# A gate projection by Strassen's algorithm on pairs of batches, with key and gate weights converted to float32 ahead of it

## The chip, the cores and the metric

One Trainium2 chip, of which the kernel uses one core. The time is device microseconds of one launch. TensorE (PE in the rows) multiplies matrices, VectorE (DVE), ScalarE (ACT) and GpSimd (POOL) work elementwise, and SyncE (SP) issues nearly all transfers from one queue.

## What is computed

Attention over 4 batches, 12 heads, 448 tokens and head width 64; then a mixer over tokens and channels; then the block that the change is about, here cut down:

```python
xk = mu_k * x + (1.0 - mu_k) * x_prev
xr = mu_r * x + (1.0 - mu_r) * x_prev
k = np.maximum(xk @ w_k, 0.0)
v = k * k @ w_v
r = 1.0 / (1.0 + np.exp(-(xr @ w_r)))
return (r * v).astype(np.float32)
```

`x` is 4 x 448 x 768, `x_prev` the same moved by one token. `w_r` is 768 x 768, `w_k` 768 x 1024 and `w_v` 1024 x 768. The weights arrive as 64-bit floats. The product with `w_r` is the gate, that with `w_k` the keys, that with `w_v` the values.

## The kernel before, in words

Every float32 operand of a large product is held as a high part (rounded) and a low part (the rest), and every block product is three matmuls: high by high, high by low, low by high (`mm3`, lines 542 to 544). Making the two parts, a split, costs one copy on ACT (`high`, L408, or L596 for the gate's inputs) and one subtraction on DVE (`low`, L412, or L599). A block of 64-bit weights is turned into float32 by one instruction on ACT (L357, or L277 in the attention part) and three on DVE (L362, L369 and L376, or L282, L289 and L295).

The program has two phases, each put in order by a list scheduler written out in the file (`walk`): each step carries an engine, an estimated cost, what it reads and writes and a due time, and the scheduler emits the instructions engine by engine. Nothing is reordered on the chip: each engine takes its own list, and SP's transfers go out in the order of SP's list.

- Phase 0 is attention with token mixing for 24 pairs of heads; idle PE time is filled with the first channel-mixing products (`pd`).
- Phase 1 begins with channel mixing (`ph`, `acc`). Its outputs `u` (L648) are blended with the previous token (L666 on ACT, L670 on DVE) for keys and for gate and stored to `x_d`.
- The gate follows. For each of two pairs of batches there are 14 units of 128 tokens by 384 columns (12 of whole 128-token tiles, 2 of the remaining 64 tokens of both batches), each a sum over six blocks of 128 channels: `pr`, 28 units of 18 matmuls. The inputs of a batch are loaded (L677), split in place (L596, L599), and the remaining tokens copied aside by a transfer (L706). The sigmoid (L718) reads PSUM and the result is parked in `r_d`.
- The keys (`pk`) and values (`pv`) already use Strassen's algorithm: 7 block products for 8, with sums of blocks formed on DVE (`take`, L400) before a split, and the products summed out of PSUM on DVE (L779, L858).
- Weights for the gate and keys are converted just ahead of and during the gate; those of the values are converted in channel mixing, combined, parked in `s_d` as float32 and loaded again in the keys.

The lines that set the gate's work per matmul and its size:

```python
def unit(o, n, x, w, start, stop):
    cs = slice(HALF * (n % 2), HALF * (n % 2 + 1))
    mm3(o[:, :HALF], [((x[:, 0], x[:, 1]), (w[:, 0, cs], w[:, 1, cs]))], start, stop)
...
    for p in range(B // 2):
        for n in range(14):
```

Of the kernel before, what the change touches and what calls it, by code (L numbers as in the profile page):

```python
# [10 lines left out]
F32 = mybir.dt.float32  # L11
# [9 lines left out]
def kernel(  # L21
# [66 lines left out]
    s_d = dpool.tile([28, 128, 384], F32, name="s_d")  # L88

# [31 lines left out]
    def walk(mine, rank):  # L121
# [218 lines left out]
    chain = {}  # L340

    def load64(t, key, src, n, own=None, blocks=False):
# [30 lines left out]
        def assemble():  # L373
# [5 lines left out]

        k = object()  # L380
        g = n / 384
        u = [("raw", k), (own or "tmp", k)]
        last = chain.get("last")
        chain["last"] = (("raw", k), key)
        op(t, SP, dma(128 * n * 8), load, r=[last[0]] if last else [], w=[("raw", k)], u=u[:1])
        op(
            t, ACT, 0.04 + 0.41 * g, magnitude, r=[("raw", k)] + ([last[1]] if last else []),
# [30 lines left out]

    FORMS = ("11", "s2", "12", "s3", "s1", "22", "s4")
# [3 lines left out]
    def w_place(fam, blk, i):  # L423
        return 4 * {"v": BLOCKS, "k": FORMS}[fam].index(blk) + i

# [11 lines left out]
    def v_weight(t, dt, kt):  # L437


        def get(t, blk, row, col, own=None):  # L440
            src = w_v[row * 128:(row + 1) * 128, 384 * col:384 * (col + 1)]
            return load64(t, ("wf", blk, kt), src, 384, own)

        def done(t, blk, tile):
            def store():
                nc.sync.dma_start(s_d[w_place("v", blk, kt)], tile[0]())

            op(
                t, SP, dma(128 * 384 * 4), store, r=[("wf", blk, kt)], w=[("ws", blk, kt)],
                u=[tile[1]],  # L450
            )

        def sub(t, blk, o, x, y, r):
            r = [("wf", b, kt) for b in r] + [("ws", b, kt) for b in blk[1:]]
            take(t, ("wf", blk[0], kt), r, [o[1], x[1], y[1]], o[0], x[0], y[0])

        a = get(t, "11", kt, 0, "tma")
        done(t, "11", a)
        b = get(t + dt, "12", kt, 1, "tmb")
        sub(t + dt, ("t1", "11"), a, b, a, ("12",))  # L460
        done(t + dt, "t1", a)
        c = get(t + 2 * dt, "22", kt + KF // 2, 1)
# [5 lines left out]
        d = get(t + 3 * dt, "21", kt + KF // 2, 0)  # L468
# [4 lines left out]
    def v_reload(t, dt, r):  # L473

        for n in range(28):
            blk, kt = BLOCKS[n // 4], n % 4
            tag = ("tma", "tmb")[n % 2]
            box, own = {}, (tag, ("re", n))

            def load(n=n, tag=tag, box=box):  # L480
                box["t"] = L["tv"].tile([128, 384], F32, tag=tag, name="tmp")
                nc.sync.dma_start(box["t"], s_d[n])

            op(
                t, SP, dma(128 * 384 * 4), load, r=[("ws", blk, kt)] + (r if n < 2 else [("rl64", n - 2)]),
                w=[("rl64", n)], u=[own],
            )
            split32(
                t + 2, ("W", "v", blk, kt), [("rl64", n)], [w_slot("v", blk, kt), own],
                lambda blk=blk, kt=kt: w_half("v", blk, kt), lambda box=box: box["t"],  # L490
# [3 lines left out]
    def k_weight(t, dt, q):  # L494


        def get(t, blk, row, col, own=None):
            src = w_k[384 * row:384 * (row + 1), 128 * (q + 4 * col):128 * (q + 4 * col + 1), :]
            src = src.rearrange("(c p) m w -> p c m w", p=128)
            return load64(t, ("kf", blk, q), src, 384, own, True)  # L500

        def done(t, blk, tile):
            split32(
# [4 lines left out]
        def add(t, blk, o, x, y, r, d, plus=False):  # L508
            r = [("kf", b, q) for b in r] + [("W", "k", b, q) for b in d]
            take(t, ("kf", blk, q), r, [o[1], x[1], y[1]], o[0], x[0], y[0], plus=plus)  # L510

        a = get(t, "21", 0, 1, "tma")
        b = get(t + dt, "11", 0, 0, "tmb")
        done(t + dt, "11", b)
        c = get(t + 2 * dt, "22", 1, 1)
# [7 lines left out]
        d = get(t + 3 * dt, "12", 1, 0)  # L523
# [23 lines left out]
    JA = 8  # L547
# [6 lines left out]
    def ch_weight(n, t, dt, pool):  # L554
# [6 lines left out]
    L = {}  # L561
    NB_ = KF * 2 + KD - NPRE
    bufs.update({
        "a2": KD, "a3": 2, "z": 7, "tma": 1, "tmb": 1, "rot": 2, "rp": 7,
# [3 lines left out]
    def open_late():  # L568
# [4 lines left out]
        new("a2", bufs=KD)  # L573
        new("a3", bufs=2)
        new("tv", bufs=1)
        new("zp", bufs=7)
# [73 lines left out]
    xs, rs, ks, rest, at, duo, xpool = {}, {}, {}, {}, {}, {}, {}  # L650
# [24 lines left out]
    def r_in(b, m):  # L675
        xs[1, b, m] = hl(xpool[1, b])
        nc.sync.dma_start(raw(xs[1, b, m]), x_d[1, b, m])  # L677

    def r_hi(b, m):
        part_hi(xs[1, b, m])  # L680

    def r_lo(b, m):
        part_lo(xs[1, b, m])
# [4 lines left out]
    def unit(o, n, x, w, start, stop):  # L688
        cs = slice(HALF * (n % 2), HALF * (n % 2 + 1))
        mm3(o[:, :HALF], [((x[:, 0], x[:, 1]), (w[:, 0, cs], w[:, 1, cs]))], start, stop)  # L690

    def tokens(n):
        return slice(128 * (n % 6 // 2), 128 * (n % 6 // 2 + 1))

    def bank(p, n):
        return f"acc{(14 * p + n) % KD}"

    def new_bank(p, n):
        rs["p", p, n] = L["acc"].tile([128, 512], F32, tag=bank(p, n), name="pr")

    def gate_rest(p, i, c):
        if ("x", p, c // 3) not in rest:
            rest["x", p, c // 3] = hl("a3")
        o = rest["x", p, c // 3][:, :, 128 * (c % 3):128 * (c % 3 + 1)]
        rest[1, p, c] = o
        nc.sync.dma_start(  # L706
            o[:, :, 64 * i:64 * i + 64].bitcast(F32), xs[1, duo[p][i], c][:, :, 384:].bitcast(F32)
        )
# [7 lines left out]
    def gate_out(p, n):  # L716
        rs[p, n] = L["rp"].tile([128, S], F32, tag="r", name="r")
        nc.scalar.activation(rs[p, n][:, :HALF], rs["p", p, n][:, :HALF], AF.Sigmoid)  # L718

    def gate_store(p, n):  # L720
        nc.sync.dma_start(r_d[p, n], rs[p, n][:, :HALF])
# [154 lines left out]
    def channel_mixing():  # L876
# [3 lines left out]
        W0, W1 = 150, 6  # L880
        V0, V1, K0, K1 = 140, 22, 40, 20
# [32 lines left out]
        for t, (b, kind, j) in enumerate(beats):  # L914
# [15 lines left out]
            if b != B - 1 and j < JA:  # L930
                op(
                    t - 3.2 * BEAT, SP, dma(SB), h_load, b, j, r=[("h_d", b, j), seen[-4]],
# [42 lines left out]
        GU, VU = 3.15, 4.2  # L975
        T3 = T2 + 14 * GU * B // 2
        N2 = 2 * KF * BEAT + 14 * VU
        at_w = {}
        for c in range(KD):
            key = ("r", c)  # L980
            at_w[key] = free_slots[c]
            weight(T2 - W0 + W1 * c, W1 / 2, at_w[key], w_r, False, c, key)
        r_slots, k_slots = free_slots[:KD], free_slots[KD:KD + 14]
        t1_slot.append(free_slots[KD + 14])
        u2_slots.extend((free_slots[KD + 15], r_slots[0]))
        for i in range(14):
            w_use["k", i] = (k_slots[i], ("W", "k", i))
        v_slots = r_slots[1:] + k_slots[:9]
        for i in range(14):
            w_use["v", i] = (v_slots[i], ("W", "v", i))  # L990
        RING = [t1_slot[0]] + k_slots[9:] + u2_slots
        KP = 7 * 4 * 3 * 0.61
        T4 = T3 + 2 * KP
        for q in range(4):
            v_weight(T2 - V0 + V1 * q, V1 / 4, q)
        for q in range(4):
            k_weight(T2 - K0 + K1 * q, K1 / 4, q)
        v_reload(T4 - 80, 2.2, [("W", "k", f, q) for f in FORMS for q in range(4)])

        rounds = [(1, b) for b in batches] + [(0, b) for b in batches]  # L1000
        gone = [
            ("ch1", batches[-1], KC - 1, KD - 1), ("c2", batches[-1], KC - 1, 0),
            ("gl", 0, 5), ("gl", 0, 11), ("gl", 1, 5),
        ]
        for n, (i, b) in enumerate(rounds):
            if i:
                xpool[i, b] = ("ue", "a2")[n % 2]
            t0 = T2 + 7 * GU * n if i else T3 + KP * (n - B) // 2
            for m in range(KD):
                need = [("x_d", i, b, m)]  # L1010
                if i or at[b][0] == 0:
                    need.append(gone[min(n, B)])
                else:
                    need.append(("km", 0, "s1", 0, 0))
                if not i:
                    t = T3 + KP * at[b][0] - 35 + 2 * m + at[b][1]
                    x = ("ue", "kx", at[b][0], m)
                    op(t, SP, dma(SB), k_in, b, m, r=need, w=[("yt", i, b, m)], u=[x])
                    continue
                t = t0 - 190 + 3 * m  # L1020
# [758 lines left out]
```

## Time and profile before

| | us |
|---|---|
| three runs | 906.22, 906.80, 911.61; median 906.8 |
| the profiled execution | 906.09, of which 904.1 are the span from the first to the last instruction |
| attention (with the first channel-mixing products) | 0 to 343 |
| channel mixing | 343 to 605.5 |
| gate | 605.5 to 692.9 |
| keys | 692.9 to 797.1 |
| values and the end | 797.1 to 904.1 |

The page counts 892.8 us of the span as busy on PE, 628.4 on DVE and 507.7 on ACT; its lines of forty digits give PE 9 in every slice but the first and the last, and the granted TensorE clock as 9 (full) in all of them. A matmul's busy time overlaps the next one's, so the pace of the matmuls has to be read from their starts.

### The profile page before, as it was taken

To read this page: it belongs to the slowest core of one execution; us is meant where nothing else is said; L and a number is where in the kernel's file an instruction comes from. 1 tells how busy PE (TensorE), PEld (TensorE's weight loads), DVE (VectorE), ACT (ScalarE), POOL (GpSimd) and SP (SyncE) were. 2 spreads that over 40 slices of the span, in tenths; PEclk is the share of its full clock that TensorE was granted. 3 is DMA by queue.
4 is the path that set the end of the run, shared out by engine and by line. 5 is a ranking of instruction groups with operands and counts; after the bars stand their busy time and mean duration, and the time that the engine had idled before them with its cause. 6 is when DMAs were issued, how large, how long until landed. Compare 5 with 4: busy or idle time off the path is not lost.

```text
span 904.1 us, 15752 instructions
## 1 busy us (share of the span) xinstructions
PE 892.8 (99%) x5340; PEld 802.9 (89%) x5340; DVE 628.4 (70%) x1568; ACT 507.7 (56%) x1205; POOL 47.8 (5%) x125
## 2 busy tenths in 40 slices
PE   7999999999999999999999999999999999999997
PEld 4688888888888889999999999999999999999997
DVE  6899997683576436887986557479723676888773
ACT  7988886674667444545554324366524576753330
POOL 1302111110101000000000000000000000000000
PEclk9999999999999999999999999999999999999999
DMA  9646755533242103666785785748762444576642
GB/s 189 171 122 162 213 165 165 151 83 93 69 133 63 51 32 113 186 186 231 254 293 195 252 295 184 228 141 282 232 226 90 154 164 141 189 231 194 181 144 62
DMA packets 174129, 151.66 MB, mean 168 GB/s; under 512 B 87584, under 2 KB 166944, under 8 KB 174048
## 3 DMA queue, kind: packets, MB, share of 16 engines
q1 hardware_dynamic: 173120, 150.42, 55.0%
q8 instruction: 42, 0.69, 0.3%
q10 hardware_dynamic: 928, 0.23, 0.1%
q14 instruction: 39, 0.32, 0.1%
HBM read 103.16 MB, written 45.88 MB: 165 GB/s over the span
## 4 chain that ended last, share of the span: by engine, by line
PE 94%; ACT 3%; DVE 1%; DMA 1%; issue 0%; SPq 0%
PE acc L544 6%; PE acc L542 6%; PE acc L543 6%; PE pv L1467 5%; PE pe L1451 4%; PE ph L542 4%; PE ph L544 4%; PE ph L543 4%; PE pk L544 4%; PE pk L543 4%; PE pk L542 4%; PE pv L544 4%; PE pv L543 4%; PE pv L542 4%; PE ps L1382 3%; PE pd L542 3%
## 5 line engine op out<-in xcount | busy, mean ns | idle before, releaser
L1410 ACT ACTIVATE e<-ms,nm 112x336 f32<-112x336 f32 (+3 forms) x192 | 100.5, 530 | 12.5 <-DVE nm L1394 11.7
L543 PE MATMUL acc<-a,w 128*128 128x448 f32 x288 | 105.2, 365 | 0.0
L542 PE MATMUL acc<-a,w 128*128 128x448 f32 x288 | 105.2, 365 | 0.0
L544 PE MATMUL acc<-a,w 128*128 128x448 f32 x288 | 105.2, 365 | 0.0
L1394 DVE CUSTOM_DVE_ANT_0 ms<-ps,mask 112x448 f32<-112x448 f32 (+3 forms) x192 | 76.7, 442 | 27.3 <-PE ps L1382 22.4
L542 PE MATMUL pv<-wv,kk 128*128 128x384 f32 x196 | 65.5, 334 | 0.0
L544 PE MATMUL pv<-wv,kk 128*128 128x384 f32 x196 | 65.5, 334 | 0.0
L543 PE MATMUL pv<-wv,kk 128*128 128x384 f32 x196 | 65.5, 334 | 0.0
L599 DVE TENSOR_TENSOR a<-a 128x448 fp32r<-128x448 f32 x84 | 51.0, 627 | 19.1 <-ACT a L596 19.0
L246 ACT COPY et<-pe 112x448 f32<-112x448 f32 x104 | 50.9, 540 | 21.5 <-PE pe L1451 21.4
L543 PE MATMUL pk<-a,wk 128*128 128x448 f32 x168 | 61.8, 368 | 0.0
L544 PE MATMUL pk<-a,wk 128*128 128x448 f32 x168 | 61.8, 368 | 0.0
L542 PE MATMUL pk<-a,wk 128*128 128x448 f32 x168 | 61.8, 368 | 0.0
L596 ACT CAST a<-a 128x448 fp32r<-128x448 f32 x84 | 46.0, 567 | 24.7 <-DMA a<-h_d 20.2
L1451 PE MATMUL pe<-ident,e 112*112 112x112 f32 x480 | 57.6, 261 | 0.9 <-ACT qt L1352 0.5
L542 PEld LDWEIGHTS acc<-a,w 128*128 128x128 f32 x288 | 54.1, 188 | 4.3
L543 PEld LDWEIGHTS acc<-a,w 128*128 128x128 f32 x288 | 54.1, 188 | 4.3
L544 PEld LDWEIGHTS acc<-a,w 128*128 128x128 f32 x288 | 54.1, 188 | 4.3
L542 PE MATMUL pd<-a,w 128*128 128x448 f32 x144 | 57.4, 399 | 0.0
L408 ACT CAST kk<-a 128x512 fp32r<-128x512 f32 x49 | 30.2, 620 | 48.4 <-PE pv L544 41.7
L1451 PEld LDWEIGHTS pe<-ident,e 112*112 112x112 f32 x480 | 49.3, 133 | 8.6 <-issue 2.0
L543 PE MATMUL pr<-w,a 128*128 128x384 f32 x168 | 56.1, 334 | 0.0
(137 smaller groups left out, 2226.9 us busy)
## 6 DMA issues: line engine op xcount, KB each, us to landing
raw<-in_moe_w_ch_dram SPq DMA_DIRECT2D x48, 384.0 KB, 3.4
x_d<-t SPq DMA_DIRECT2D x48, 224.0 KB, 3.5
a<-x_d SPq DMA_DIRECT2D x48, 224.0 KB, 4.5
a<-u_d SPq DMA_DIRECT2D x36, 224.0 KB, 3.8
raw<-in_moe_w_v_dram SPq DMA_DIRECT2D x16, 384.0 KB, 3.9
raw<-in_moe_w_k_dram SPq DMA_DIRECT2D x16, 384.0 KB, 4.2
a<-a_d SPq DMA_DIRECT2D x24, 256.0 KB, 4.4
vn<-in_v_dram SPq DMA_DIRECT2D x48, 112.0 KB, 2.7
```

The source lines that it names most:

```text
L246: nc.scalar.copy(o, i) if by == ACT else nc.vector.tensor_copy(o, i)
L408: nc.scalar.copy(dest()[0], src())
L542: nc.tensor.matmul(o, lh, rh, start=start and i == 0, stop=False, skip_group_check=skip)
L543: nc.tensor.matmul(o, lh, rl, start=False, stop=False, skip_group_check=skip)
L544: nc.tensor.matmul(o, ll, rh, start=False, stop=stop and i == n - 1, skip_group_check=skip)
L596: nc.scalar.copy(t[:, 0], raw(t))
L599: nc.vector.tensor_sub(t[:, 1], raw(t), t[:, 0].bitcast(F32))
L1382: nc.tensor.matmul(T["s", j, c], T["q"][r, x, qc], T["k"][r, y, :n], start=i == 0, stop=i == 2,)
L1394: nc.vector.tensor_tensor_reduce(out=ms[:, :n], in0=T["s", j, c], in1=mask[:, S - n:], scale=-0.125, scalar=BIG, op0=ALU.add, op1=ALU.min, ...
L1410: nc.scalar.activation(T["e", j][:, eoff[c]:eoff[c + 1]], T["ms", j, c][:, :n], AF.Exp, bias=T["nm"][:, j, c:c + 1], scale=-1.0, accum_out ...
L1451: nc.tensor.transpose(pe[:CP, o + (c - kc) * CP:o + (c - kc + 1) * CP], T["e", j][:, eoff[c] + kc * CP:eoff[c] + (kc + 1) * CP], ident[:CP ...
L1467: nc.tensor.matmul(T["pv"][64 * j:64 * j + 64, kc * CP:S], T["vn"][:, kc, j, :], T["et"][:, o:o + S - kc * CP], start=kc == 0, stop=kc == 2,)
```

## The change

The gate is computed on pairs of batches by Strassen's algorithm. A product of two batches' rows with `w_r` cut into two by two blocks takes 7 block products. The 14 tiles of 128 tokens form 7 groups of two ("quads"): three from the first pair of batches, three from the second, and one of the remaining 64 tokens of all four. Each block product of a quad is three blocks of 128 channels, so 9 matmuls; a pass over three quads is 27 matmuls per product. The inputs of a pair are loaded as plain float32, summed on DVE (`take`, now L409), and each of the seven forms is split into its own tile (L417 on ACT, L421 on DVE). Five of the seven products need a sum out of PSUM on DVE (`r_sum`, L831), the first a copy on ACT (`r_copy`, L828). The pool of split tiles (`a2`) has 8 in place of 6, that of the blended tiles (`z`) 6 in place of 7, and four single tiles (`tma` to `tmd`) serve the weights in place of two.

24 blocks of weights (8 of the gate's 12, all 16 of the keys') are converted in the attention part by `convert`, from the eleventh pair of heads on and with a late due time, and stored as float32 in `c_d`; later they are fetched from there. The last four blocks of the gate's weights are still converted in channel mixing. Half of the keys' weight forms (14 of 28) are made earlier than before, parked in `t_d` and loaded again late (`reload`).

The core of the diff:

```diff
+    t_d = dpool.tile([14, 128, 384], F32, name="t_d")
+    c_d = dpool.tile([24, 128, 384], F32, name="c_d")
...
+    def convert(t, fam, blk, i, gate):
+        n = early[fam, blk, i] = len(early)
+        tile, own = load64(t, ("cf", n), block_src(fam, blk, i), 384, None, fam == "k", gate)
+        def store():
+            nc.sync.dma_start(c_d[n], tile())
+        op(t, SP, dma(128 * 384 * 4), store, r=[("cf", n)], w=[("cd", n)], u=[own])
...
-        "a2": KD, "a3": 2, "z": 7, "tma": 1, "tmb": 1, "rot": 2, "rp": 7,
+        "a2": A2, "z": 6, "tma": 1, "tmb": 1, "tmc": 1, "tmd": 1, "rot": 2, "rp": 7,
...
+    def r_bank(n, q, where):
+        if n == REST:
+            return "rot"
+        return f"acc{q + (3 if where == 'b' else 0)}"
+    def rmm(n, f, q, c):
+        blk, where, start, stop = PRODUCTS[f]
...
+        mm3(
+            rp_[n, q, where][:, :HALF], [((x[0][:, cs], x[1][:, cs]), w_half("r", blk, c))],
+            start=start and c == 0, stop=c == KD // 2 - 1, skip=not start,
+        )
+    def r_sum(n, q, o, where, x):
+        nc.vector.tensor_add(r_temp(n, q, o), rp_[n, q, where][:, :HALF], r_temp(n, q, x))
...
-    def gate(p, n, c):
-        if c == 0:
-            new_bank(p, n)
-        x = xs[1, duo[p][n // 6], c][:, :, tokens(n)] if n < 12 else rest[1, p, c]
-        unit(rs["p", p, n], n, x, weights["r", c]["t"], c == 0, c == KD - 1)
...
+        def x_tile(gone):
+            n = len(xs_free)
+            xs_free.append(gone)
+            return xs_free[n - KD] if n >= KD else [("ch1", batches[-1], KC - 1, KD - 1)]
...
+                    m, x = len(cols) * half + c, ("ue", "rx", n, len(cols) * half + c)
+                    gone = x_tile([("ro", n, f, c) for f in (("s4", "22") if half else ("s2", "s3"))])
...
+                add(t, "s1", ld((0, 1), (1, 1)), s1, a21, a22, True)
+                add(t + 0.2, "s3", made("s1") + ld((0, 0)), a21, a11, a21)
+                add(t + 0.4, "s2", made("s3") + [("ro", n, "11", c)], a11, s1, a11)
+                add(t + 0.6, "s4", made("s2") + ld((1, 0)) + [("ro", n, "12", c)], a12, a12, a11)
...
+        GATE, LOW = 10, 60
...
+        blocks = [("r", b, i) for i in (1, 2) for b in ("11", "12", "22", "21")]
+        blocks += [("k", b, i) for i in range(4) for b in ("21", "11", "22", "12")]
+        for i, x in enumerate(blocks):
+            g = GATE + i * (NP * B - 1 - GATE) // len(blocks)
+            convert(tp(g) + LOW, *x, [("xlo", g)])
```

What stands where on the engines that PE waits for shows at two places. The first is DVE right behind the last channel-mixing output (`u`, the row that ends at the first gate matmul). Before, the splits of the gate's inputs and the making of the keys' weights stand there:

```order
L648 TENSOR_TENSOR u_7249<-acc5_6889,u_7249 128x448
...
L369 TENSOR_SCALAR tmp_7348<-tmp_7348 128x384
L599 TENSOR_TENSOR a_7371<-a_7371 128x448
L400 TENSOR_TENSOR tmp_7269<-tmp_7291,tmp_7269 128x384
L412 TENSOR_TENSOR wk_7199<-tmp_7322,wk_7199 128x384
L400 TENSOR_TENSOR tmp_7291<-tmp_7322,tmp_7291 128x384
L412 TENSOR_TENSOR wk_7206<-tmp_7269,wk_7206 128x384
L376 SCALAR_TENSOR_TENSOR tmp_7348<-raw_7296,tmp_7348 128x384
```

Behind the change it is splits of Strassen forms (`a_7531` and so on), sums out of PSUM (`pr`) and the blends, 62 rows from here to the split of the third column of the second pair's first form:

```order
L734 TENSOR_TENSOR u_7448<-acc5_7059,u_7448 128x448
L421 TENSOR_TENSOR a_7531<-a_7289,a_7531 128x448
L756 SCALAR_TENSOR_TENSOR t_7460<-u_7419,mu_r_75,t_7460 128x448
L756 SCALAR_TENSOR_TENSOR t_7472<-u_7427,mu_r_75,t_7472 128x448
L421 TENSOR_TENSOR a_7569<-a_7304,a_7569 128x448
...
L409 TENSOR_TENSOR s1_7900<-a_7633,a_7848 128x448
L409 TENSOR_TENSOR a_7633<-a_7633 128x448
L831 TENSOR_TENSOR x_7587<-pr_7653,x_7587 128x384
L409 TENSOR_TENSOR a_7633<-s1_7900,a_7633 128x448
...
L831 TENSOR_TENSOR x_7644<-pr_7832,x_7644 128x384
L421 TENSOR_TENSOR a_7902<-a_7748,a_7902 128x448
```

The conversions of 64-bit weights (L362, L369, L376) are gone from this place, and the forms of the second pair (`s1_7900` on) stand ahead of the split `a_7902` that its first product needs.

The second place is SP's list in the gate. Before, the loads of the third batch stand together, with the raw weights:

```order
L349 DMA raw_7296<-in_moe2_w_k_dram 128x3x256
L677 DMA a_7302<-x_d_78 128x448
L677 DMA a_7308<-x_d_78 128x448
L677 DMA a_7314<-x_d_78 128x448
L677 DMA a_7317<-x_d_78 128x448
L677 DMA a_7334<-x_d_78 128x448
L349 DMA raw_7339<-in_moe2_w_k_dram 128x3x256
```

Behind the change the second half of the second pair's inputs (`a_7848`, `a_7863`, `a_7875`, two transfers each) stands behind stores of the first pair's gate (`r_d`):

```order
L759 DMA x_d_78<-t_7792 128x448
L839 DMA r_d_79<-w_7758 128x384
L774 DMA a_7848<-x_d_78 128x448 x2
L774 DMA a_7863<-x_d_78 128x448 x2
L774 DMA a_7875<-x_d_78 128x448 x2
L839 DMA r_d_79<-w_7781 128x384
```

These tiles are taken over from the first pair, so each pair of loads also waits until the first pair's fourth form (`s4`) of the same column has been split.

## Rows read from the trace of the kernel before

**Rows 1.** The page's part 4: shares of the chain that ended last, by engine.
```profile
PE 94%; ACT 3%; DVE 1%; DMA 1%; issue 0%; SPq 0%
```

**Rows 2.** Busy time by stage: stretch, length; PE, PEld, DVE, ACT, POOL; clock, DMA share, GB/s.
```profile
174.00:343.00 169.00, 169.00 (x1223) 143.42 (x1220) 97.93 (x327) 105.06 (x294) 10.80 (x27) 1.00 0.28 82
343.00:572.00 229.00, 229.00 (x1132) 212.26 (x1131) 166.14 (x355) 102.56 (x201) 4.56 (x36) 1.00 0.68 220
...
605.50:692.90 87.40, 87.40 (x505) 87.39 (x505) 53.56 (x108) 43.42 (x88) 0.50 (x5) 1.00 0.64 209
692.90:797.10 104.20, 104.20 (x506) 94.66 (x506) 70.08 (x125) 69.50 (x137) 0.00 (x0) 1.00 0.53 170
```

**Rows 3.** What PE waited for, whole span: first and last of six rows.
```profile
PE pt L1348 <- DMA kn<-in_k_dram: 4.0, 1, 4.0
...
PE ps L1373 <- DVE nm L1394: 0.2, 1, 0.2
```

**Rows 4.** PE in order of time at both ends of the gate: start, length, instruction.
```profile
605.32 0.36 PE L544 MATMUL acc<-a,w 128*128 128x448 f32 x1
605.52 0.34 PE L542 MATMUL pr<-w,a 128*128 128x384 f32 x1
...
692.73 0.33 PE L544 MATMUL pr<-w,a 128*128 128x384 f32 x1
692.90 0.36 PE L542 MATMUL pk<-a,wk 128*128 128x448 f32 x1
```

**Rows 5.** The page's part 5: one of the gate's three matmul lines.
```profile
L543 PE MATMUL pr<-w,a 128*128 128x384 f32 x168 | 56.1, 334 | 0.0
```

**Rows 6.** DVE in order of time around the gate's start: start, length, instruction, count.
```profile
602.68 3.66 DVE L648 TENSOR_TENSOR u<-acc,u 128x448 f32<-128x448 f32 x6 [1.18 <-DMA a<-x_d]
606.26 2.76 DVE L599 TENSOR_TENSOR a<-a 128x448 fp32r<-128x448 f32 x5
...
612.07 0.55 DVE L412 TENSOR_TENSOR wk<-tmp,wk 128x384 fp32r<-128x384 f32 x1
612.54 0.55 DVE L400 TENSOR_TENSOR tmp<-tmp 128x384 f32<-128x384 f32 x1
...
616.41 1.27 DVE L670 SCALAR_TENSOR_TENSOR t<-u,mu_r,t 128x448 f32<-128x448 f32 x2
```

**Rows 7.** DVE in the gate by line and form: count, busy us, mean ns, idle before.
```profile
L599 DVE TENSOR_TENSOR a<-a 128x448 fp32r<-128x448 f32 x18 | 10.5, 619 | 2.1 <-ACT a L596 2.1
...
L376 DVE SCALAR_TENSOR_TENSOR tmp<-raw,tmp 128x384 int32<-128x384 int32 x9 | 5.0, 555 | 0.2
L670 DVE SCALAR_TENSOR_TENSOR t<-u,mu_k,t 128x448 f32<-128x448 f32 x6 | 4.0, 678 | 0.1
...
L362 DVE TENSOR_SCALAR tmp<-tmp 128x384 f32<-128x384 f32 x9 | 3.2, 354 | 3.1 <-ACT tmp L357 3.1
```

**Rows 8.** The same in the values: a sum out of PSUM.
```profile
L858 DVE TENSOR_TENSOR u<-pv,x 128x384 f32<-128x384 f32 x14 | 7.8, 556 | 7.4 <-PE pv L544 7.4
```

**Rows 9.** ACT in the gate by line and form.
```profile
L596 ACT CAST a<-a 128x448 fp32r<-128x448 f32 x15 | 8.0, 561 | 0.1
```

**Rows 10.** SP's queue in order of time: six loads of gate inputs.
```profile
569.84 3.36 SPq L677 DMA_DIRECT2D a<-x_d  x6
```

**Rows 11.** Transfers issued in the gate: KB each, median us to landing.
```profile
a<-x_d SPq DMA_DIRECT2D x25, 224.0 KB, 5.1
```

**Rows 12.** Transfers issued at the end of channel mixing, the same columns.
```profile
a<-x_d SPq DMA_DIRECT2D x12, 224.0 KB, 3.8
```

**Rows 13.** The tile of natural keys in attention: first and last start, time to landing.
```profile
L1348 PE MATMUL pt<-ident,kn x96: 257/259/421, 4.0 to 289.0; 112*128 112x112 f32 x96
L1337 SPq DMA_DIRECT2D kn<-in_k_dram x47: 312/481/2298, 0.7 to 274.0; - x47
...
DMA to landing us min/median/max: 2.0/3.4/5.0
```

**Rows 14.** What SP's queue waited for from 174 to 343: total, times, longest.
```profile
SPq L1697 <- ACT he L1694: 52.9, 12, 8.4
```

More of the change, by code (lines that the diff above doesn't have):

```diff
@@ L338, in weight, with load64 @@
             t += dt
-    chain = {}
-    def load64(t, key, src, n, own=None, blocks=False):
+    chain, DEEP = {}, 2
+    def load64(t, key, src, n, own=None, blocks=False, gate=()):
         box = {}
@@ L378, in assemble @@
             )
+        held = [] if own else [chain[x] for x in ("tma", "tmb", "tmc", "tmd") if x in chain]
+        if own:
+            chain[own] = key
         k = object()
@@ L382, in load64 @@
         u = [("raw", k), (own or "tmp", k)]
-        last = chain.get("last")
-        chain["last"] = (("raw", k), key)
-        op(t, SP, dma(128 * n * 8), load, r=[last[0]] if last else [], w=[("raw", k)], u=u[:1])
+        last = chain.setdefault("last", [])
+        was = last[-DEEP] if len(last) >= DEEP else None
+        last.append((("raw", k), key))
+        op(t, SP, dma(128 * n * 8), load, r=list(gate) + list(was[:1] if was else []), w=[("raw", k)], u=u[:1])
         op(
-            t, ACT, 0.04 + 0.41 * g, magnitude, r=[("raw", k)] + ([last[1]] if last else []),
+            t, ACT, 0.04 + 0.41 * g, magnitude, r=[("raw", k)] + ([was[1]] if was else []) + held,
             w=[("mag", k)], u=u,
@@ new lines, in r_in, with r_s1 @@
+    def r_in(n, m, i):
+        if n != REST:
+            nc.sync.dma_start(r_block(n, m, i), x_d[1, duo[n][i], m])
+            return
+        o = r_block(n, m, i).rearrange("p (c t) -> p c t", t=128)
+        for e in range(2):
+            src = x_d[1, duo[i][e], 3 * m:3 * m + 3, :, 384:]
+            nc.sync.dma_start(o[:, :, 64 * e:64 * e + 64], src.rearrange("c p t -> p c t"))
+    def r_s1(n, c):
+        if (n, "s1") not in rx:
+            rx[n, "s1"] = pools[t1_slot[0]].tile([128, 2, 768], F32R, tag=t1_slot[0], name="s1")
+        t = rx[n, "s1"].rearrange("p a b -> p (a b)").bitcast(F32)
+        return t[:, :HALF] if n == REST else t[:, S * c:S * (c + 1)]
@@ new lines, in r_form @@
+    def r_form(n, f, c):
+        if (n, f, c) not in ro:
+            ro[n, f, c] = hl("a2")
+        t = ro[n, f, c]
+        return (t[:, 0, :HALF], t[:, 1, :HALF]) if n == REST else parts(t)
+    def r_bank(n, q, where):
[4 more added lines that the diff above has]
+        blk, where, start, stop = PRODUCTS[f]
+        if start and c == 0:
+            b = r_bank(n, q, where)
+            rp_[n, q, where] = (
+                L["rot"].tile([128, 512], F32, tag="r", name="pr") if b == "rot"
+                else L["acc"].tile([128, 512], F32, tag=b, name="pr")
+            )
+        x = r_form(n, f, 0 if n == REST else c)
+        cs = slice(128 * (c if n == REST else q), 128 * (c if n == REST else q) + 128)
+        mm3(
+            rp_[n, q, where][:, :HALF], [((x[0][:, cs], x[1][:, cs]), w_half("r", blk, c))],
+            start=start and c == 0, stop=c == KD // 2 - 1, skip=not start,
+        )
@@ new lines, in r_temp @@
+    def r_temp(n, q, name):
+        if (n, q, name) not in rz:
+            if n == 0 and name in "xu":
+                slot = r_room[name]
+                if (n, slot) not in rz:
+                    rz[n, slot] = pools[slot].tile([128, 2, 768], F32R, tag=slot, name="x")
+                t = rz[n, slot].rearrange("p a b -> p (a b)").bitcast(F32)[:, HALF * q:]
+            elif name in "xu":
+                t = ytile(name, "zp")
+            else:
+                t = L["rp"].tile([128, S], F32, tag="r", name=name)
+            rz[n, q, name] = t[:, :HALF]
+        return rz[n, q, name]
@@ L716, in gate_out @@
[L716 to L721, printed above, removed]
     def gate_load(p, n):
@@ new lines, in channel_mixing @@
+        RP = 7 * (KD // 2) * 0.53
+        T3 = T2 + 7 * RP
+        KP = 7 * 4 * (KD // 2) * 0.61
+        T4 = T3 + 2 * KP
+        r_slots, k_early = free_slots[:11], free_slots[12:22]
+        t1_slot.append(free_slots[11])
+        u2_slots.extend(r_slots[4:6])
+        late = [w_place("k", f, q) // 2 for f, q in LATE[6::2]]
+        k_slots = [None] * 14
+        for i, x in enumerate([i for i in range(0, 14, 2)] + [i for i in range(1, 14, 2) if i not in late]):
+            k_slots[x] = k_early[i]
```

392 lines of the change are left out of this document (249 added, 143 removed), and 5 rows, old and new, of the table NUDGES.

## The prediction, written before the change was run

> **What bounds the kernel now.** The first view is the chain that ended last: 94% of it is PE [rows 1], so a gain must take work off PE, or a loss must make PE wait. The second is the table by stage: from 174 us on PE is busy in the whole of every stretch shown, at a granted clock of 1.00 [rows 2], while DVE is busy 98 of 169 us in late attention, 166 of 229 in channel mixing, 54 of 87 in the gate. Since busy time hides gaps, the third view is what PE waited for: six rows between a 4.0 us wait for the first keys and one of 0.2 us [rows 3], about 6 us in all, every one at lines of attention. The fourth is PE in order of time at both ends of the gate: the last channel-mixing matmul starts at 605.32 and the gate's first at 605.52, the last at 692.73 and the keys' first at 692.90 [rows 4]. So the gate takes 692.90 - 605.52 = 87.4 us for 3 x 168 = 504 matmuls [rows 5], one every 87.4 / 504 = 0.1734 us, with no gap at either end. PE alone bounds it.
>
> I count time from the gate's first matmul, called zero.
>
> **What the change takes off PE.** Seven quads of 7 products of 9 matmuls are 441 for 504. Their shape is the same, 128 x 128 by 384 columns, so the pace should be too: 441 x 0.1734 = 76.5 us, 10.9 less. Against the profiled execution of 906.1 that is 895.2. The median of the runs is 0.7 above that execution, which I add at the end.
>
> **What it puts on DVE in the gate.** First the price of a row. Five splits of 448 columns take 2.76 us together and one lasts 0.62 [rows 6, 7], so they start (2.76 - 0.62) / 4 = 0.535 apart; two rows of 384 columns start at 612.07 and 612.54, 0.47 apart though each lasts 0.55; two blends start 1.27 - 0.68 = 0.59 apart [rows 6, 7]. A sum out of PSUM of 384 columns lasts 0.556 [rows 8], like the other 384-wide rows, so I put it at 0.47 too (an estimate).
>
> In the new order, from the last output `u` to the last sum of the gate, DVE has 138 rows: 66 of 448 columns, 12 blends, 60 of 384 columns (35 sums out of PSUM, 25 others). 66 x 0.535 + 12 x 0.59 + 60 x 0.47 = 70.6 us, in a gate of 76.5. Before, it was busy 53.6 of 87.4 [rows 2]. DVE goes from 61% to over 90%, and that is where the change can fail. The gate's inputs were split once (24 tiles); now there are 49 splits of forms and 28 sums of blocks, and 35 sums of products that did not exist. What is saved are raw conversions (two rows of 0.35 and one of 0.56 for a block [rows 7]).
>
> Two splits are tight. The 26th row is that of the third column of form `s3`. The 26 rows take 8 x 0.535 + 9 x 0.59 + 9 x 0.47 = 13.8 us. The first row behind `u` starts 0.74 after zero (606.26 [rows 6]), so it ends at 14.6; PE wants it at its 90th matmul, 89 x 0.1734 = 15.4. It is in time by 0.8.
>
> The 62nd is `a_7902`, the third column of the second pair's first form. 28 x 0.535 + 12 x 0.59 + 22 x 0.47 = 32.4, plus 0.74: 33.1. PE wants it at its 198th matmul, at 34.2: 1.0 to spare, if DVE never waits. It will, twice. Row 49 sums product `22` of the second quad, which PE ends at 26.5, so rows 49 on cannot be before 27.2. Row 50 needs the second pair's inputs `a_7848`, whose tile is free once `s4` of that column is split, the 42nd row, at 23.0. SP issues such loads 0.56 apart (six in 3.36 [rows 10]), so the second of the two leaves at 23.7; landing took 3.8 us at the end of channel mixing [rows 12] and 5.1 in the gate [rows 11]. Row 50 thus starts between 27.5 and 28.8, and the 13 rows from it to `a_7902` take 9 x 0.535 + 4 x 0.47 = 6.7: it ends between 34.2 and 35.5, so PE is late by 0 to 1.3 us. I take 1.1, near the upper end, since the 5.1 is from the same stage, though the keys' raw loads of 384 KB no longer fall into it. Later splits have 3 us and more, in the last quad 12, since work on PE outlasts that on DVE. The three sums that free the banks for the second pair lie among the 62 rows and are due later or at the same time.
>
> ACT makes one copy for each of 62 splits (0.56 [rows 9]) and has 47 other rows, sigmoids of 384 columns for the most part; at 0.56 for each that is at most 61 of 77 us, under DVE's load and off the path.
>
> **What it puts elsewhere.** Attention gets 24 conversions, each one row on ACT, three on DVE (0.35 + 0.35 + 0.56 [rows 7]), a raw load and a store: 30 us on DVE and some 13 on ACT. DVE has 71 us free from 174 to 343 alone, ACT 64, and the transfer engines are 0.28 busy there [rows 2]. PE's own instructions are the same 2352 before the first `acc`, with a few exchanged places. I cost it at nothing; what hides it is this free time and the lead of the loads below. Channel mixing loses the gate's conversions and gains sums, splits and stores; in its last three batches DVE's rows grow by some 6 us of 175, with 63 free in the row of 229 us [rows 2]: nothing. In the keys, eight blocks of weights arrive only after the gate's weights are done with. The first of them is for the fourth product, and a product there lasts 104.2 / 14 = 7.4 us [rows 2], so they have 22 us for loads that land in 5.1: nothing.
>
> **Sum.** 906.1 - 10.9 + 1.1 = 896.3 against the profiled execution, **897.0** against the median.
>
> **Rivals.**
> *DVE falls behind in the gate.* If a row on DVE started only when the one before it had ended, the 62 rows would take 28 x 0.62 + 12 x 0.68 + 22 x 0.555 = 37.7 us, `a_7902` would end at 38.5 and PE would stand 4.3 us: 900.2 against the median. Rows of 0.55 that start 0.47 apart speak against it. [...] The likelier way to the same place is inputs that land later than 5.1, or a blend that waits for one of only six `z` tiles, with DVE's list held up behind it; 3 to 7 us lost give 899 to 903.5. Together 0.20.
>
> *Attention starves for its loads: slower.* The 24 stores of converted blocks stand in SP's one list, each waiting for DVE's last row of a low-priority conversion, and the loads of queries and keys stand behind them. SP already waited 52.9 us for 12 other stores, up to 8.4 at a time [rows 14], and PE lost nothing: the last keys were loaded at 274.0, land in 3.4, and were first used near 289.0 [rows 13], a lead of about 11 us. If the new waits use up this lead, each of the 13 pairs from the eleventh on makes PE wait. From 1.5 us a pair on, 20 us, the whole is over 9 us slower: 906.8 - 9.8 + 20 = 917. I give it 0.06.
>
> *The gain is paid back in small sums* in attention's redrawn order, or where eight `a2` tiles serve both channel mixing's end and the first forms: 5 to 10 us lost, 902 to 907. Against it stands that every other stage has a quarter of DVE free. 0.10. That the product count is cut but the pace of a matmul grows belongs here: at the 0.20 us of a 448-column matmul (605.32 to 605.52 [rows 4]) 441 would take 89 us and nothing would be won; with 384 columns I see no reason.
>
> *More than the sum*: attention's new order ends earlier too, under 895. 0.04.
>
> **Numbers.** The forecast, 895 to 899, has 0.60. The range of 894.5 to 904 holds it, the first rival and part of the third and fourth. About 1% of 906.8 is what a measurement of this kernel can tell from no change, so the bound for faster is 897.7, which the forecast straddles: of its 0.60 I put 0.46 under it, with the 0.04 of the last case 0.50 for faster. Within 1%: the rest of the forecast and the first and third rivals, 0.44. Slower 0.06.
>
> **What would show it.** Right: 441 matmuls `pr`, first to next stage 76.5 to 78.5 us; DVE over 85% busy in the gate; one gap on PE of about 1 us some 34 us after its start, ended by DVE's split or by nothing else; attention and channel mixing ending within 1 us of 343 and 605.5. Wrong: a gap of over 3 us there, or several; PE waiting for `kn` or `qn` after the eleventh pair; a gate that starts later than 607.

## The result, and the profile after

Four executions, the profiled one among them, have a median of **897.35 us** (896.24 to 897.68) against 907.07 for the kernel before: a ratio of 0.988, interval 0.985 to 0.991. Two later sets on other chips gave 897.83 against 906.85 (0.990, 0.988 to 0.991) and 897.73 against 906.95 (0.990, 0.988 to 0.991). So the change takes 9.0 to 9.7 us off; the forecast was 897.0. The range held it. That the change saves time is clear, since no interval reaches beyond 0.991; whether it is "faster by over 1%" is as open as the prediction left it, since the bound of 897.7 lies between these medians.

The profiled execution is the fastest of its four, 896.24 us with a span of 894.4. First its page, part 4, shares of the chain that ended last [rows 1]:

```profile
PE 89%; ACT 5%; DVE 3%; DMA 2%; issue 1%; SPq 0%; ACTq 0%; DVEq 0%
```

The table by stage, in the columns of [rows 2]:

```profile
174.00:343.00 169.00, 168.76 (x1223) 143.03 (x1220) 119.64 (x383) 111.81 (x307) 15.72 (x37) 1.00 0.53 160
343.00:572.00 229.00, 228.92 (x1130) 211.81 (x1129) 164.73 (x347) 100.69 (x197) 4.54 (x36) 1.00 0.69 225
...
605.90:683.30 77.40, 77.15 (x443) 76.41 (x442) 71.53 (x138) 51.41 (x106) 0.59 (x6) 1.00 0.65 209
683.30:787.40 104.10, 104.10 (x506) 94.56 (x505) 77.17 (x139) 73.06 (x144) 0.00 (x0) 1.00 0.60 192
```

The gate is 77.4 us long for 87.4, the keys 104.1 as before. DVE is busy 71.5 us of the 77.4 with the 138 rows that were counted, 92% for 61%. In late attention it has gone from 98 to 120 us, and the transfer engines from 0.28 to 0.53. From 343 to 572 us, in channel mixing, next to nothing has moved.

PE in order of time, as in [rows 4]: start, length, instruction. The two ends of the gate and the two places in it where a start comes late:

```profile
605.75 0.37 PE L630 MATMUL acc<-a,w 128*128 128x448 f32 x1
605.96 0.34 PE L628 MATMUL pr<-wr,a 128*128 128x384 f32 x1
...
639.96 0.34 PE L629 MATMUL pr<-wr,a 128*128 128x384 f32 x1
640.36 0.44 PE L630 MATMUL pr<-wr,a 128*128 128x384 f32 x1
640.64 0.34 PE L628 MATMUL pr<-wr,a 128*128 128x384 f32 x1
...
676.38 0.34 PE L630 MATMUL pr<-wr,a 128*128 128x384 f32 x1
676.90 0.44 PE L628 MATMUL pr<-wr,a 128*128 128x384 f32 x1 [0.19 <-DVE u L831]
677.18 0.34 PE L629 MATMUL pr<-wr,a 128*128 128x384 f32 x1
...
683.14 0.33 PE L630 MATMUL pr<-wr,a 128*128 128x384 f32 x1
683.32 0.36 PE L628 MATMUL pk<-a,wk 128*128 128x448 f32 x1
```

A matmul's length (0.33 to 0.44) reaches past the next one's start, so the distance of two starts is what is read here. It is 0.173, and never over 0.20, everywhere but at 639.96 (0.40, and 0.28 behind it) and 676.38 (0.52, and 0.28): 0.34 and 0.46 us lost. The first is the low-part matmul of the split `a_7902`, 34.0 us after the gate's start; the second is the first matmul of a product in the last quad, which wants a bank that DVE has yet to read.

What DVE does ahead of both, in order of time, idle time in brackets:

```profile
632.70 0.56 DVE L831 TENSOR_TENSOR x<-pr,x 128x384 f32<-128x384 f32 x1 [0.33 <-PE pr L630]
633.17 0.62 DVE L409 TENSOR_TENSOR s<-a 128x448 f32<-128x448 f32 x1
...
635.61 0.63 DVE L409 TENSOR_TENSOR s<-a 128x448 f32<-128x448 f32 x1 [0.16 <-DMA a<-x_d]
...
639.22 0.55 DVE L831 TENSOR_TENSOR x<-pr,x 128x384 f32<-128x384 f32 x1
639.69 1.15 DVE L421 TENSOR_TENSOR a<-a 128x448 fp32r<-128x448 f32 x2
...
674.75 0.63 DVE L409 TENSOR_TENSOR a<-a 128x448 f32<-128x448 f32 x1 [0.80 <-DMA a<-x_d]
675.29 1.09 DVE L421 TENSOR_TENSOR a<-a 128x384 fp32r<-128x384 f32 x2
676.30 0.55 DVE L831 TENSOR_TENSOR u<-pr,x 128x384 f32<-128x384 f32 x1
```

SP sends the second half of the second pair's inputs out at:

```profile
629.32 2.69 SPq L774 DMA_DIRECT2D a<-x_d  x6
```

632.70 is the sum of product `22`, the row that the prediction called 49; with it 13 rows stand ahead of the split at 639.69, and one of them, at 635.61, waits shortly for its input. At 674.75 a row of the *keys* waits 0.80 us for its load, and the sum that frees PE's bank (676.30) stands behind it and two splits.

A third place is the step from attention into channel mixing. PE, then ACT:

```profile
343.36 0.36 PE L630 MATMUL ph<-a,w 128*128 128x448 f32 x1
343.80 0.47 PE L628 MATMUL ph<-a,w 128*128 128x448 f32 x1
344.11 0.36 PE L629 MATMUL ph<-a,w 128*128 128x448 f32 x1
```
```profile
343.21 0.54 ACT L1913 ACTIVATE he<-pd 128x448 f32<-128x448 f32 x1
```

The matmul at 343.80 is first in its bank and begins when ACT has read the bank's old content (343.21 + 0.54). This costs 0.34 us, in each of the eight profiles with this order of lists.

**The account** of the two profiled executions: gate 87.39 - 77.36 = 10.03 less, which is 63 matmuls (10.92) less the gate's lost 0.89 (0.80 in the two gaps, the rest in single starts a little late); attention 0.10 and the step 0.34 more; the end of the program 0.10 and the time outside the span 0.16 less. 10.03 - 0.44 + 0.26 = 9.85 = 906.09 - 896.24. Other executions of the same kernel reach the gate later, as e1 shows.

### The profile page after: what moved, and what is told of

Read it like the earlier page. It is cut to its first block, busy times and chain, and to the rows that moved or that the text cites. A ratio compares the mean times of both kernels' runs of the same rounds, so it can differ in the third digit from the quotient of the medians.

```text
span 894.4 us, 15883 instructions
## 1 busy us (share of the span) xinstructions
PE 882.5 (99%) x5277; PEld 791.3 (88%) x5277; DVE 680.3 (76%) x1670; ACT 525.0 (59%) x1240; POOL 52.9 (6%) x138
## 4 chain that ended last, share of the span: by engine, by line
PE 89%; ACT 5%; DVE 3%; DMA 2%; issue 1%; SPq 0%; ACTq 0%; DVEq 0%
PE acc L629 7%; PE acc L628 7%; PE acc L630 7%; PE pe L1670 5%; PE pv L1686 5%; PE ph L628 4%; PE ph L630 4%; PE ph L629 4%; PE pk L629 4%; PE pk L628 4%; PE pk L630 4%; PE pv L628 4%; PE pv L630 4%; PE pv L629 4%; PE pd L628 3%; PE ps L1601 3%
## 5 line engine op out<-in xcount | busy, mean ns | idle before, releaser
L1613 DVE CUSTOM_DVE_ANT_0 ms<-ps,mask 112x336 f32<-112x336 f32 (+3 forms) x192 | 76.7, 441 | 20.1 <-PE ps L1601 17.6
L417 ACT CAST kk<-a 128x512 fp32r<-128x512 f32 x49 | 30.3, 622 | 48.1 <-PE pv L630 40.5
L628 PE MATMUL pd<-a,w 128*128 128x448 f32 x144 | 57.5, 399 | 0.0
L417 ACT CAST a<-a 128x448 fp32r<-128x448 f32 (+1 forms) x78 | 41.8, 559 | 21.3 <-PE pk L630 10.1
L628 PE MATMUL ph<-a,w 128*128 128x448 f32 x144 | 52.7, 366 | 0.1
L630 PE MATMUL pd<-a,w 128*128 128x448 f32 x144 | 52.7, 366 | 0.0
```

The lines of the kernel that those rows point to most:

```text
L417: nc.scalar.copy(dest()[0], src())
L628: nc.tensor.matmul(o, lh, rh, start=start and i == 0, stop=False, skip_group_check=skip)
L630: nc.tensor.matmul(o, ll, rh, start=False, stop=stop and i == n - 1, skip_group_check=skip)
L1613: nc.vector.tensor_tensor_reduce(out=ms[:, :n], in0=T["s", j, c], in1=mask[:, S - n:], scale=-0.125, scalar=BIG, op0=ALU.add, op1=ALU.min, ...
```

## The experiments

What a run is compared with is the changed kernel, unless the text says otherwise. e5 to e8 are single executions.

Early conversion without Strassen's algorithm was not run, nor the change without the parked weight forms of `t_d`. In the gate of before PE had no gap ([rows 4]), so that conversions taken out of it had nothing to win there.

### e1 and e10: the changed kernel again

> The changed kernel as it is, for comparison with the others of this set. 897.3 us, +-0.7; the same two gaps of PE in the gate, 0.34 us some 34 us after its start and 0.46 us some 70 us after it, since each engine's list is fixed. If the gaps were chance (the rival), they would sit elsewhere or be absent this time.

> The changed kernel as it is, beside e9 and e11. 897.4 us, +-0.7; gate 77.3 to 77.8, start of the gate 606.0 to 607.8 by the transfers of attention.

897.83 and 897.73 us. The gaps sit at the same two matmuls, but they are not of the same size: the first 0.83 and 0.68 us for 0.34, the second 0.42 and 0.29 for 0.46. The gate begins at 607.8 and 607.7 for 606.0. The lists are fixed; what differs at the first gap is when a transfer lands. Why the gate begins later is not shown. DVE ahead of the first gap in e1:

```profile
636.65 0.61 DVE L409 TENSOR_TENSOR a<-s,a 128x448 f32<-128x448 f32 x1
637.91 0.63 DVE L409 TENSOR_TENSOR s<-a 128x448 f32<-128x448 f32 x1 [0.64 <-DMA a<-x_d]
```

The wait that was 0.16 is 0.64 here, and the gap grows by as much. Over eight profiles with these lists up to the gate (after, e1, e2, e5, e7 to e10), the gate's first matmul lies between 605.96 and 607.77, at 606.9 in the mean; in the two with the lists of before (the profile before and e6) at 605.5 and 606.2. Between the means lie 1.1 us, not the 0.44 of the one profile. This is rough: the two profiles with the lists of before lie 0.7 apart, and the eight of the change spread over 1.8. The medians give a second estimate: in e1's set the change saves 9.02, while its gate saves 9.62 and what stands behind the values' start some 0.2, so 0.8 went in front; the same sum gives 0.6 to 1.2 for the result, e2, e9 and e10. So the front of the program pays about 1 us for the change.

### e2 and e9: are the two gaps a matter of order?

```diff
-                        t0 + step * i - 9 + 0.5 * c, ("ro", n, f, c), r + gone,
+                        t0 + step * i - (14 if n == 1 and i == 0 else 9) + 0.5 * c, ("ro", n, f, c), r + gone,
...
-                t = t0 - 14 + 0.5 * c
+                t = t0 - (14 if n else 10) + 0.5 * c
```

(e9 has 8 in place of the 10.)

> Two due times are changed: the first form of the second pair is split 5 us earlier in the list (14 for 9 ahead), and the sums for the keys' inputs 4 us later (10 for 14 ahead). Theory (two gaps from the order of DVE's list: 13 rows behind a sum that waits for PE's own product, and a sum out of PSUM that stands behind a keys' row waiting for its load): both gaps close, the gate takes 76.5 to 76.6 us for 77.4, the whole 0.8 to 0.9 less than the changed kernel in the same set. Rival (DVE is full in the gate, 93%, and any order has to pay for it somewhere): the gaps move to other forms and the gate stays at 77.2 or more.

> As e2, with the sums for the keys' inputs due 8 us ahead of the keys for 14 (e2: 10). In the list the row that waits for the keys' load now stands behind the sum that frees the bank for PE, not two rows ahead of it. Theory: both gaps are closed, the gate takes 76.5 to 76.7 us, the keys and values stay at 104.2 and 101.8, and the whole is 0.8 to 1.3 less than the changed kernel in the same set. Rival (DVE is full, the wait turns up elsewhere): 77.1 or more in the gate, or a gap at the keys' start.

e2: 897.06 us, gate 77.15. The first gap is closed. The second is not, and has 0.62 us: my 4 us did not move the waiting row behind the sum, which the list would have told. e9 has them in the right order:

```profile
675.58 0.62 DVE L421 TENSOR_TENSOR a<-a 128x448 fp32r<-128x448 f32 x1
676.11 0.56 DVE L831 TENSOR_TENSOR u<-pr,x 128x384 f32<-128x384 f32 x1
676.66 0.63 DVE L421 TENSOR_TENSOR a<-a 128x448 fp32r<-128x448 f32 x1
677.20 0.62 DVE L409 TENSOR_TENSOR a<-a 128x448 f32<-128x448 f32 x1
```
```profile
607.00:683.50 76.50, 76.50 (x442) 76.48 (x442) 71.87 (x139) 51.38 (x106) 0.59 (x6) 1.00 0.66 212
```

The sum (676.11) now stands ahead of the row that takes the load (677.20). The gate takes 76.47 us, which is 441 x 0.1734 to the hundredth, with DVE as busy as before. So a DVE at 94% costs nothing where its list has the right order: the rival of e2 falls. The whole is 897.02 us for e10's 897.73. That is the direction and the size, 0.7, a little under the 0.8 to 1.3 expected, but the single runs of both (896.27 to 897.94, 895.88 to 898.87) overlap; the gate's 1.04 us is shown by the traces, not by the medians. e9 has the lowest median of the versions that compute the whole, and cannot be told apart from e2.

### e7 and e8: what sets the time of the first gap?

```diff
-        nc.vector.scalar_tensor_tensor(t, y, mu[:, m:m + 1], t, op0=ALU.mult, op1=ALU.add)
+        if i == 1 or b != B - 2:
+            nc.vector.scalar_tensor_tensor(t, y, mu[:, m:m + 1], t, op0=ALU.mult, op1=ALU.add)
```
```diff
-            (eng.tensor_add if plus else eng.tensor_sub)(o(), x(), y())
+            for _ in range(2 if twice else 1):
+                (eng.tensor_add if plus else eng.tensor_sub)(o(), x(), y())
...
-                add(t, "s1", ld((0, 1), (1, 1)), s1, a21, a22, True)
+                add(t, "s1", ld((0, 1), (1, 1)), s1, a21, a22, True, twice=n == 1)
```

> The six blends for the keys' inputs of the last batch are left out on DVE (the keys of that batch are then of the previous token alone). They stand among the 48 rows ahead of the sum of product 22 (row 49). Theory (row 49 waits for PE's product, and the 13 rows from it to the split set the gap): the gap at 34 us stays, 0.2 to 0.4 us, though DVE has 3.5 us less to do ahead of it. Rival (the sum of all rows sets it): the gap is gone and the split comes some 3 us earlier.

> The three sums s1 of the second pair are made twice; each stands behind row 49 and ahead of the split that PE waits for, and waits for its first copy, so it adds about 0.65 us. Theory (no slack is left behind row 49): the gap at 34 us grows from 0.34 by 1.7 to 1.95 us, all of it lost for good, the gate takes 79.0 to 79.4. Rival (DVE's idle time, 6 us in the gate, takes it up): the gap grows by less than 0.6.

e7 by stage, from the gate's start to row 49, then that row on DVE (here L832):

```profile
606.70:633.40 26.70, 26.70 (x155) 26.69 (x155) 23.34 (x44) 19.69 (x39) 0.59 (x6) 1.00 0.72 240
```
```profile
633.47 0.56 DVE L832 TENSOR_TENSOR x<-pr,x 128x384 f32<-128x384 f32 x1 [0.47 <-PE pr L630]
```

The changed kernel has 26.12 us and 50 rows in that stretch. e7 does six rows less and row 49 still starts 26.7 us after the gate's first matmul, for PE's product is not done before. The gap is 0.28 us. So six rows fewer ahead of row 49 gain next to nothing. More rows there were not tried, and they would not be free for long: DVE waits only 0.33 us at row 49 in the changed kernel. What stands behind row 49 does matter. e8:

```profile
640.61 0.34 PE L630 MATMUL pr<-wr,a 128*128 128x384 f32 x1
643.34 0.45 PE L631 MATMUL pr<-wr,a 128*128 128x384 f32 x1 [2.39 <-DVE a L422]
```

The time lost at this place is 2.67 us, 2.3 more than before; 1.95 of it are three rows of 0.65, and 0.34 a later load (a wait of 0.50 for 0.16). The whole was 899.39, the gate 79.57, a little over what I expected, for the load.

### e5 and e6: how far off is DVE in each gate?

```diff
+    def mm2(o, terms, start=True, stop=True, skip=False):
+        for (lh, ll), (rh, rl) in terms:
+            nc.tensor.matmul(o, lh, rh, start=start, stop=False, skip_group_check=skip)
+            nc.tensor.matmul(o, ll, rh, start=False, stop=stop, skip_group_check=skip)
```

> The changed kernel with one of the three matmuls of each block product (high by low) left out in the gate, 294 for 441; every other list stays. Theory (DVE is the next bound of the changed gate, at 71.5 us busy of 77.4): PE could do it in 51.0 us, but the gate takes 70 to 75, 2 to 7 us less than 77.4 where PE's work falls by 25.5; the whole is 890 to 895. Rival (DVE has room): 51 to 60 us, the whole 872 to 880.

> The kernel before with the same third of the gate's matmuls left out, 336 for 504. Theory (the old gate had DVE free for 34 of 87 us): 58.3 to 62 us for the gate, 25 to 29 less, the whole 877 to 882. Rival (something else was just behind PE in the old gate too): 70 us or more.

e5, then e6 with its keys behind it:

```profile
606.60:680.10 73.50, 59.80 (x295) 57.46 (x294) 70.44 (x137) 50.08 (x105) 0.59 (x6) 0.86 0.67 218
```
```profile
606.20:666.80 60.60, 59.47 (x337) 58.02 (x336) 45.77 (x94) 39.14 (x81) 0.49 (x5) 1.00 0.83 271
666.80:775.70 108.90, 104.60 (x506) 96.36 (x506) 77.38 (x139) 72.21 (x143) 0.00 (x0) 0.97 0.56 177
```

The new gate gives back 3.8 us of PE's 25.5, the old one 26.8 of 29.1: DVE was far off and is now right behind PE. In e5 it is busy 70.4 of 73.5 us, and PE's waits end on DVE for 6.9 us and on ACT for 6.8. PE's mean granted clock is 0.86 there (0.50 from 621.8 to 626.0, 0.53 from 642 to 647); with DVE busy nearly throughout, this can hardly have set the time. e5's 893.04 is as expected. e6's 884.74 is not (877 to 882): its keys took 4.7 us more, with a wait of 4.3 for the split of one of their first inputs:

```profile
PE pk L543 <- DVE a L412: 4.3, 1, 4.3
```

The gate that ended early found the next stage not ready.

### e3: without the early conversion

```diff
-            convert(tp(g) + LOW, *x, [("xlo", g)])
+            pass
```

> The 24 conversions in attention are left out; the same blocks are converted from 64-bit floats where their sums are made, in channel mixing and the gate, as before the change. Theory (the early conversion is what keeps DVE's list short enough in the gate; in attention it costs 0.4 us): DVE's list in the gate is longer by raw conversions, and by counts of rows times their distance (0.27, 0.27, 0.47) the worst split comes 7 us too late, so the gate takes 83 to 87 us, attention and the step to channel mixing win back up to 0.4, and the whole is 903 to 907. Rival (DVE has room for them in channel mixing, the conversion is beside the point): 896.5 to 898.5.

911.18 us (ratio to before 1.006, interval 1.004 to 1.009): beyond my range on the side of the theory, 13.4 more than e1. By stage, late attention, then the gate, then a piece of it:

```profile
174.00:343.00 169.00, 168.38 (x1224) 142.27 (x1222) 97.48 (x325) 103.86 (x291) 11.71 (x28) 1.00 0.28 79
...
607.90:697.60 89.70, 81.67 (x442) 79.27 (x442) 85.22 (x174) 58.74 (x123) 0.59 (x6) 0.96 0.63 198
...
622.20:626.40 4.20, 4.20 (x16) 4.20 (x17) 4.20 (x8) 3.13 (x6) 0.20 (x2) 0.61 0.66 201
```

DVE has 174 rows in the gate for 138 and is busy 85 of 89.7 us. PE's longest sum of waits in the gate is for its splits:

```profile
PE pr L630 <- DVE a L421: 5.8, 5, 3.3
```

PE loses 13.3 us: 9.3 in seven gaps, 1.5 in a stretch of ten matmuls that start 0.32 apart (the row from 622.20 holds it: granted clock 0.61), the rest mostly in other starts behind gaps; from 653 to 661 the granted clock is 0.79. With the lists that the scheduler draws without the early conversion, Strassen's 63 matmuls less lose to the kernel before. The 0.4 that I expected attention to win back did not come: the gate starts at 607.9.

### e4, e11 and e12: is a conversion free in attention?

e4 repeats each conversion (a second `load64` and a store), e11 only its load and its store, as further steps. e12 adds to the instructions of the 24 steps that are there:

```diff
+            if twice:
+                nc.sync.dma_start(e_d[key[1]], block_src("v", "11", key[1] % 4))
+                nc.sync.dma_start(f_d[key[1]], block_src("v", "22", key[1] % 4)[:, :192])
...
-            nc.vector.tensor_scalar(
+            for _ in range(1 + 2 * twice):
+                nc.vector.tensor_scalar(
```

> Each of the 24 blocks is converted twice in attention and stored a second time to a place that nothing reads: 24 more raw loads, conversions and stores. Theory (free time of DVE and of the transfer engines hides a conversion there): DVE is busy some 21 us more of the 169 us from 174 to 343 (about 140), PE loses less than 1 us more, and the whole is 897.3 to 898.5. Rival (the conversions already stand at the edge, SP's list holds up the loads of queries and keys): each pair from the eleventh on waits, 5 to 20 us more, 902 to 917.

> As e4, but of the second conversion only its two transfers are left: 24 more raw loads and 24 more stores, no more rows on ACT and DVE. e4 took 5.6 us more than the changed kernel, against my expectation. Theory now (the price of a conversion in attention is DVE's: its rows delay the maxima, copies and splits that PE waits for): 0 to 1.5 us more than the changed kernel. Rival (the price is SP's list or the transfer engines): 3 to 6 us more, as e4.

> e4 and e11 added steps, and with more steps the scheduler also draws another order of attention's whole list. Here the lists stay those of the changed kernel, and each of the 24 conversions only becomes heavier where it stands: one more row on ACT, three more on DVE (30 us by lengths), and two copies from DRAM to DRAM of 384 and 192 KB in place of a second load and store. Theory now (the 5.6 us of e4 and 8.3 us of e11 are the redrawn order; free time does hide a conversion): 0 to 1.5 us more than the changed kernel's 897.7. Rival (transfers or DVE's rows themselves are the price): 4 to 8 us more, 902 to 906.

903.46, 906.02 and 917.8 us (ratios to before 0.9965, 0.9985 and 1.012; intervals 0.995 to 0.998, 0.997 to 1.000 and 1.010 to 1.014): 5.6, 8.3 and 20 more. Each of my three theories fell, and the last two results lie beyond the rivals' ranges too. From 174 to 343 us, e4, e11 and e12:

```profile
174.00:343.00 169.00, 166.72 (x1210) 140.52 (x1207) 134.02 (x431) 119.56 (x326) 16.61 (x37) 1.00 0.72 211
```
```profile
174.00:343.00 169.00, 165.90 (x1201) 136.93 (x1197) 116.21 (x387) 111.89 (x310) 7.31 (x13) 1.00 0.74 223
```
```profile
174.00:343.00 169.00, 158.00 (x1126) 128.08 (x1125) 137.11 (x429) 115.95 (x316) 15.19 (x31) 0.99 0.69 213
```

DVE is never busier than 137 of 169 us, the transfer engines never over 0.74, and still PE stands: 11 us of this stretch in e12. e11 has DVE busy 116 us here where the changed kernel has 120, so DVE's time alone is not the price. (e11's redrawn lists also move 18 rows of attention from GpSimd, 11 of them to DVE and 7 to ACT.) The two largest of PE's waits in e12 (us in total, times, longest), and one of ACT's:

```profile
PE pe L1679 <- ACT et L253: 2.7, 3, 2.1
PE pn L1713 <- DVE xT L253: 2.5, 3, 1.4
```
```profile
ACT tmp L369 <- DMA c_d<-tmp: 6.0, 2, 4.1
```

PE waits for plain attention rows of ACT and DVE (`et`, `xT`), and on ACT a conversion waits up to 4.1 us for the store that frees its tile, with such rows behind it. The longest of both waits are one chain, on ACT and then on PE:

```profile
223.67 1.12 ACT L369 ACTIVATE tmp<-raw 128x384 f32<-128x384 f32 x2 [4.15 <-DMA c_d<-tmp]
224.70 0.95 ACT L253 COPY et<-pe 112x448 f32<-112x448 f32 x2
```
```profile
225.26 0.59 PE L1679 MATMUL pe<-ident,e 112*112 112x112 f32 x4 [2.06 <-ACT et L253]
```

That is a list held up. How much of the 20 us this way costs, and how much the load on the transfer engines or SP's list, the three runs do not tell apart; e4 and e11, where the scheduler knew of the added steps and drew another order, lost less. What they do settle: the free time that [rows 2] shows in attention did hide the 24 conversions (about 1 us for the whole front of the program), and did not hide 24 more in any of the three forms tried.

## Why the prediction was right, and where it was not

**PE's term was exact.** 441 matmuls at 0.1734 are 76.47 us, and e9 takes 76.47. Keys and values keep their pace.

**DVE's count was right.** 138 rows, 70.6 us put down, 71.5 busy. The price per row held: the splits from 639.69 start 0.53 apart though each is 0.62 long. Had each row started only when the one before it had ended, as in the first rival, PE would have stood 4.3 us at the first gap by the prediction's sum. It stood 0.34 to 0.83. In e8, where a second sum writes the tile that the first has just written, the second starts 0.65 after the first: the two take 1.27 us, one alone 0.62.

**The tight split was the right one.** The gap came 34 us after the start, between the bounds of 0 and 1.3 (I took 1.1), and mostly for the reason given: row 49 at 26.7 us (PE's product was put down to end at 26.5), 13 rows from it to the split, the loads sent out from 23.4 on. One step was off: row 50, which the prediction had waiting for its load until 27.5 to 28.8, started at 27.2 right behind row 49. The load that came late was the next column's, four rows on, by 0.16 to 0.64 us, so that the 1.1 was mis-sized. e7 and e8 show that row 49 and what stands behind it set it, e1 and e10 that the loads make its size.

**The second gap was missed.** "Later splits have 3 us and more, in the last quad 12" holds for splits; but PE also waits for sums that free a bank, and the last quad works in banks that it shares. The prediction weighed three such sums at the second pair and none in the last quad. The 0.1 to 0.6 us of this gap (0.1 in e7) came from a keys' row waiting for a load, the list held up behind it: the first rival's mechanism, at a tenth of its price.

**"I cost it at nothing" was too low for attention**, by about 1 us (0.44 in the one profile): 0.34 in the step to channel mixing, where only "a few exchanged places" were granted, and the rest in attention. One of the signs named for being wrong, a gate that starts later than 607, shows in four of the eight profiles. SP did wait behind the new stores, as the starvation rival had it, and the keys' loads still kept their lead, as in [rows 13] and [rows 14]:

```profile
SPq L447 <- DVE tmp L381: 17.4, 9, 6.1
```
```profile
L1567 PE MATMUL pt<-ident,kn x96: 257/259/422, 4.0 to 292.7; 112*128 112x112 f32 x96
L1556 SPq DMA_DIRECT2D kn<-in_k_dram x47: 312/482/2223, 0.7 to 268.8; - x47
```

The last load of keys goes out 24 us ahead of its use, for 15 before. e12 came to that rival's 917 us by another way: the keys' loads kept their lead there too (last load at 287.2, last use at 312.2), and the waits were for ACT's and DVE's rows. "What hides it is this free time" was the weakest sentence of the prediction, since busy time is not what runs out there.

**The sum was nearer than its terms, which is luck.** 1.1 us for the first gap was too much, nothing for the second gap and for attention too little; together 1.1 was put down against 0.9 to 1.3 in the gate and about 1 ahead of it. Two small gains that were not put down, 0.10 us at the end of the program and 0.16 outside the span in the two profiled executions, go the other way. So the medians have 9.0 to 9.7 us for the 9.8 forecast.

**What the prediction did not see** is that the early conversion carries the change. It priced the attention part as a cost near zero, and did not ask what the gate would be without it: some 12 us longer, as e3 shows.

## What to carry to other kernels

Where work is taken off the bounding engine, count the rows of the next one to the last, in the order of its list, and look for the row that cannot start before a given moment: what stands ahead of it costs nothing as long as it is done by then (with six rows fewer in e7 the gap was still 0.28 us), and each row behind it is paid in full (three rows of 0.65 in e8 cost 1.95 us). Check not only the operands that the bounding engine needs but also the reads that free its banks, and any row ahead of them that waits for a transfer. An engine's idle share says that work was hidden, not that more can be: a second helping of the same conversions cost 6 to 20 us where the first cost about 1.

## What the runs showed of the hardware that was not expected

- PE's granted clock was lower behind some gaps. In e3, PE stood 3.5 us between its starts at 618.52 and 622.18; from 623.2 to 626.4 the starts of its 384-column matmuls then lie 0.32 apart, for 0.173 before the gap, and the mean granted clock from 622.2 to 626.4 is 0.61, for 1.00 from 607.9 to 618.5. From 653 to 661 in the same gate, with PE busy 6.3 of 8.0 us, it is 0.79. In e6, after a wait of 4.3 us, 448-column matmuls start 0.373 apart, for 0.20 from 676.6 on, and the clock from 671.4 to 676.2 is 0.50. In e8, after a wait of 2.39 us, the next starts lie 0.28 and 0.18 apart. The gap of 3.5 us in e3 cost 5.2 us with what came behind it, half as much again.
- With the same lists, the matmul ahead of the gate's first gap starts at 639.96 us in the result's profile and at 641.77 in e1's, while from 5 to 350 us no single wait of PE is over 0.9 us in either; a difference of 1 us between two profiles says nothing about a change in front of the gate.
